# Loads of quads 7 and 8 and half of batch 3's values issued in chunk 1's MLP stage, with an output ring of four

## The chip, the cores and the metric

The kernel runs on one core of one Trainium2 chip. The metric is the device time of one execution in microseconds (us); lower is better. Five engines work side by side and meet through semaphores: PE (TensorE, matmul; its weight loads are a row of their own, PEld), DVE (VectorE), ACT (ScalarE), POOL (GpSimd) and SP (SyncE), which here only issues DMAs. DMAs issued by POOL travel on the queue that the profile calls q0, those of SP on q1; q8 and q14 carry instructions. All use the core's 16 DMA engines.

## The reference

Decayed causal attention for 8 batches x 8 heads, 576 positions, head size 64, followed by an MLP with tanh GELU over all 4608 tokens:

```python
scores = scale * np.matmul(q, k.transpose(0, 1, 3, 2))
cum = np.cumsum(np.log(np.clip(f, 0.0001, 1.0)), axis=-1)
scores = np.where(causal, -1e9, scores + cum[:, :, :, None] - cum[:, :, None, :])
attn = softmax(scores)                 # over the keys
x = matmul(attn, v)  ->  (4608, 512)   # heads side by side
h = x @ w_in                           # 512 x 2048
out = gelu_tanh(h) @ w_out             # 2048 x 512, float32
```

## The kernel before, in words

Attention is done by quads: quad i is four heads of one batch, so batch b is quads 2b and 2b+1, 16 quads in all. The MLP is done by chunks of 512 tokens, nine of them (0 to 8). Chunk c is interleaved with the attention of the two quads that come next: chunk 1 with quads 5 and 6, chunk 2 with quads 7 and 8, and so on.

The order of all work is written by hand. `FRONT` is a string of words for the set-up, chunk 0 and chunk 1; `TABLES[c]` is the like for chunks 2 to 8. `run` and `play` walk over the words, and each word calls one function that emits its instructions, each to the queue of its engine. Every engine works off its own queue in order; a word's place in the string fixes its place in that queue, and semaphores do the rest. The words that matter here:

- `LK.i`, `LQ.i`: load the keys or queries of quad i into `k_c[i % 2]` or `q_c[i % 2]`, turning float32 into bf16, 288 KB written; one DMA, issued by POOL (L190).
- `TK.i`, `TQ.i`: DVE transposes them into `kT`, `qT` (L196). The load of quad i+2 goes into the same buffer as that of quad i, so it waits for the transpose of quad i.
- `LV.b.half`: the values of four heads of batch b, five DMAs on SP (L167), four of 128 KB and one of 64 KB, into half of `v_nat[b % 2]`; packets of 256 bytes. `LX.b.half` is the same issued by POOL. `LV` in a table loads a whole batch (b = c+2), five DMAs of up to 256 KB.
- `@LK.6` and the like, behind a word: it waits for that earlier load to land.
- `S.i.r`: scores of quad i, round r (PE L259, then exp on ACT, L267); `M.i.r`: its causal mask on POOL (L273); `m`: mask by product on DVE (L302); `D.i`: denominators; `V.i.x`: attention times values (L327); `VW.i`, `vw.i`: values weighted, on POOL or DVE (L213).
- `I.c.p` and `P.p`: two of the 16 blocks of the first MLP product of a chunk (PE L372, GELU on ACT L379); `U`, `G`: sums of weights and of GELU outputs on DVE (`w_out` as seven half-size products instead of eight); `F.c.n`, `f.c.n`: the next n of the 112 matmul steps of the second product of chunk c (L508), `O` the rest of the chunk before.

A stage of chunk c from 1 to 5 therefore has an MLP part of some 14 us, in which PE runs 64 long matmuls of 512 columns, and an attention part of some 20 us with short matmuls of many weights: about 700 matmuls and as many weight loads in the stage.

In `FRONT`, chunk 1's MLP stage runs from `I.1.0` to `G.1.1.2`. The words around the change, as they stand before:

```
... LQ.7 VW.4 ... I.1.5 U.1 LV.3.0@LQ.7 m.4.2.2 TK.6 G.0 M.4.0 I.1.2 I.1.3 U.3 ...
... CL.5 m.5.2.2 LQ.8 S.6.0 f.1.10 M.5.1 ... m.6.2.3 LK.7 LK.8 CL.6 LX.3.1@LK.6
```

Stage 2 (`TABLES[2]`) begins with `Y O.512 P.0 P.1 TK.q3 TQ.q3 LK.q5 LQ.q5 TK.q4 TQ.q4 LK.q6 LQ.q6 LV`, where q3 is quad 7, q4 quad 8, q5 quad 9 and q6 quad 10.

Outputs leave through tiles `o_st` of the pool `ostage` (three buffers): DVE adds a PSUM bank and a kept part into `o_st` (L533), SP stores it (L521). The last chunk writes its last corner in pieces (L546, L548). `f_sb` holds the forget gates for the set-up: loaded by SP (L589), clipped on DVE (L605), logarithm on ACT (L606), transposed on PE (L611), and not used after that. `g2` is one of three buffers of sums of GELU outputs (`gsum` in the profile), first written by `G.0` of chunk 1 (L489).

Of the kernel before, what the change touches and what calls it, by code (L numbers as in the profile page):

```python
# [8 lines left out]
FP32 = mybir.dt.float32  # L9
# [7 lines left out]
def kernel(  # L17
# [12 lines left out]
    B, H, S, D = q.shape  # L30
    BH = B * H
# [40 lines left out]

    FRONT = """
        TQ.0 B.2.256 TK.1 SB TR LP.2@LQ.0 B.2.128 CW S.0.0 B.5.384 B.1.256 Z TQ.1 vw.0.0 S.0.2 WI.0 LQ.2 M.0.0 B.3.384 H.1.0.1 LP.3 B.1.256 vw.1.0
        WI.1@LU.4 W H.1.1.1 WI.3 B.2.256 WI.2 H.1.0.0 M.1.0.1 D.0.0 M.1.0.0 H.0.1.1 V.0.0.0 H.0.1.0 B.2.256 M.0.1 H.1.1.0 V.0.1.0 D.1.0 H.0.3.0 B.2.128
        V.1.0.0 LX.1.1 H.0.3.1 V.1.1.0 m.0.3.2 H.1.3.0 m.0.3.4 B.1.256 VW.1.1 H.1.3.1 B.4.128 vw.0.1 D.0.1 M.1.3 S.1.2 M.1.1 LK.2 V.0.1.1 V.0.0.1 WO.0
        J.0.1 D.1.1 J.0.0 WO.1@LV.1.1 V.1.1.1 V.1.0.1 J.0.3 WO.2@WI.1 VW.3 J.1.0 WO.3 LK.3 LQ.3 J.1.1 TQ.2 J.1.3 LQ.4 LX.1.0@WO.2 TK.2 J.0.2 J.1.2 X
        LK.4 F.0.6 TK.3 B.3.256 S.2.0 LK.5 F.0.9 S.2.2 F.0.10 S.2.1 TQ.3 TQ.4 F.0.10 LV.2.0@LK.5 m.2.1 vw.2 TK.4 S.3.0 f.0.1 M.2.2 CL.2 LQ.5 M.2.0 D.2
        f.0.6 S.3.1 m.3.0 F.0.6 V.2.0 S.3.2 TK.5 LK.6 M.3.2 f.0.7 V.2.1 CL.3 S.4.1 m.3.1 LQ.6 F.0.6 TQ.5 H.4.2.1 D.3 H.4.0.1 LQ.7 VW.4 H.4.0.0 V.3.1
        v.3.0 f.0.3 H.4.2.0 CL.4 I.1.0 m.4.1 U.0 LV.2.1@LQ.5 I.1.4 TQ.6 m.4.2.3 I.1.1 I.1.5 U.1 LV.3.0@LQ.7 m.4.2.2 TK.6 G.0 M.4.0 I.1.2 I.1.3 U.3  # L80
        I.1.6 I.1.7 G.1.1.2 U.2 X F.1.16 S.5.0 f.1.26 S.5.1 D.4 M.5.0 f.1.16 S.5.2 V.4.0 m.5.2.3 f.1.10 VW.5 V.4.1 CL.5 m.5.2.2 LQ.8 S.6.0 f.1.10 M.5.1
        D.5 f.1.7 S.6.1 V.5.1 f.1.12 V.5.0 vw.6 S.6.2 m.6.1 M.6.2.2 m.6.0 m.6.2.3 LK.7 LK.8 CL.6 LX.3.1@LK.6
    """

    HOMES = {1: 0, 3: 1}
# [28 lines left out]
    """  # L114

    singles = ctx.enter_context(tc.tile_pool(name="singles", bufs=1))
    ostage_pool = ctx.enter_context(tc.tile_pool(name="ostage", bufs=3))
    snap_pool = ctx.enter_context(tc.tile_pool(name="snap", bufs=4))
    den_pool = ctx.enter_context(tc.tile_pool(name="den", bufs=1))
    rb_pool = ctx.enter_context(tc.tile_pool(name="rb", bufs=2))  # L120
# [4 lines left out]
    def many(n, shape, dtype, name):  # L125
        return [singles.tile(shape, dtype, name=f"{name}{i}") for i in range(n)]
# [11 lines left out]
    vw = many(2, [128, NT + 1, 4, D], BF16, "vw")  # L138
# [4 lines left out]
    g1, g2, g4 = many(3, [128, HF, HC], BF16, "gsum")  # L143
    u1, u2, u4 = many(3, [128, HF, HD], BF16, "usum")
    w_in_sb = singles.tile([128, N_DT, D_FF], BF16, name="w_in_sb")
    w_out_sb = singles.tile([128, N_FT, D_MODEL], BF16, name="w_out_sb")
    f_sb = singles.tile([BH, S], FP32, name="f_sb")
    logfT = singles.tile([128, NT * BH], FP32, name="logfT")
    before = singles.tile([128, (NT - 1) * BH], FP32, name="before")
    wT = singles.tile([128, NQ, NT, 4], FP32, name="wT")  # L150
# [635 lines left out]
```

## Time and profile before

| what | value |
|---|---|
| median of 3 runs | 329.81 us (329.66 to 330.34) |
| the profiled execution, its own time | 329.67 us |
| its span | 328.0 us |
| PE busy | 316.0 us (96%) |
| DVE, ACT, POOL busy | 205.3, 201.7, 110.8 us |
| instruction DMA (q8) | 42 packets, 0.69 MB |
| q0 (POOL's DMAs) | 16.58 MB, 28.3% of 16 engines' span |
| q1 (SP's DMAs) | 16.01 MB, 18.3% |

The span is the time between the first and last instruction that the profile shows; the execution's own time has 1.67 us more around it. Where a row of the profile has "idle before, releaser", the time in brackets is how long that engine had nothing to run, and the name is what ended the wait; "issue" means that nothing in the profile explains it. Queue names ending in q are the engine's sequencer, which issues DMAs and waits. Chunk 1's MLP stage begins at 67.25 us, chunk 2's at 102.01, chunk 3's at 137.11; each is the time of the stage's first matmul of line L372.

### The profile page before, as it was taken

What the parts mean: (1) busy time and instruction counts of PE and PEld (TensorE: products, weight loads), DVE (VectorE), ACT (ScalarE), POOL (GpSimd) and SP (SyncE); (2) the same over time, 40 slices, a digit from 0 to 9 for tenths busy, and PEclk for the clock granted to TensorE, in tenths of its full rate; (3) what the DMA queues carried; (4) which work ended last, traced back from release to release, by engine and by line L of the source; (5) the groups of instructions that cost most, each with busy time, mean ns of one, the idle gap of its engine ahead of it and who ended that gap; (6) DMA issues with size and microseconds to landing.
All of it is one profiled execution on the core that took longest, in us unless ns stands there. A gap on an engine that the chain in (4) does not pass through costs nothing.

```text
span 328.0 us, 11922 instructions
## 1 busy us (share of the span) xinstructions
PE 316.0 (96%) x5395; PEld 206.6 (63%) x5415; DVE 205.3 (63%) x323; ACT 201.7 (61%) x231; POOL 110.8 (34%) x155
## 2 busy tenths in 40 slices
PE   3999999999999999999999999999999999999995
PEld 1358844545776468646774587557754786687684
DVE  4586039894866864674567466636553758785772
ACT  4684677775767576668656774768666841721630
POOL 8986563510414415520644054403440140000000
PEclk9999999999999999999999999999999999999999
DMA  7999999861124990295128711661110102002012
GB/s 125 209 209 218 162 231 201 164 163 35 36 40 95 237 211 27 83 197 110 37 68 179 144 37 36 150 133 36 36 66 0 36 7 96 2 32 98 0 34 96
DMA packets 44322, 33.42 MB, mean 102 GB/s; under 512 B 27488, under 2 KB 37856, under 8 KB 44272
## 3 DMA queue, kind: packets, MB, share of 16 engines
q0 software_dynamic: 8848, 16.58, 28.3%
q1 hardware_dynamic: 35280, 16.01, 18.3%
q8 instruction: 42, 0.69, 0.9%
q14 instruction: 8, 0.07, 0.1%
q10 hardware_dynamic: 144, 0.07, 0.1%
HBM read 36.85 MB, written 9.44 MB: 141 GB/s over the span
## 4 chain that ended last, share of the span: by engine, by line
PE 91%; DMA 3%; POOL 1%; ACT 1%; DVE 1%; issue 1%; DVEq 0%; POOLq 0%; ACTq 0%
PE ps_h L372 29%; PE ps_w L508 29%; PE po L327 9%; PE ps_s L259 8%; PE ps_h L462 4%; PE pso L578 4%; DMA v_nat<-in_v_dram 3%; PE ps_cd L420 2%; PE ps_ab L420 2%; ACT pt L267 1%; PE po_m L313 1%; DMA out_dram<-o_st 1%; POOL v_nat L167 0%; PE ps_o L327 0%; DVE pt L302 0%
## 5 line engine op out<-in xcount | busy, mean ns | idle before, releaser
L267 ACT ACTIVATE pt<-ps_s 128x1024 bf16<-128x1024 f32 (+2 forms) x100 | 93.7, 988 | 39.4 <-PE ps_s L259 34.1
L372 PE MATMUL ps_h<-xT,w_in_sb 128*128 128x512 bf16 x432 | 98.0, 379 | 0.8
L379 ACT ACTIVATE gT<-ps_h 128x1024 bf16<-128x1024 f32 x56 | 57.2, 1021 | 49.1 <-PE ps_h L372 47.6
L273 POOL TENSOR_SCALAR_AFFINE_SELECT pt<-pt 128x512 bf16<-128x512 bf16 (+3 forms) x65 | 38.4, 600 | 133.2 <-ACT pt L267 132.3
L372 PEld LDWEIGHTS <-w_in_sb 128*128 128x128 bf16 x448 | 43.8, 98 | 50.1 <-issue 0.4
L508 PEld LDWEIGHTS <-gT 128*32 128x32 bf16 (+1 forms) x1247 | 51.0, 97 | 6.4 <-issue 1.7
L508 PE MATMUL ps_w<-w_out_sb,gT 128*32 128x256 bf16 (+1 forms) x1050 | 46.9, 273 | 0.0
L508 PEld LDWEIGHTS <-gsum 128*32 128x32 bf16 (+1 forms) x1256 | 38.9, 97 | 1.5 <-issue 0.2
L259 PE MATMUL ps_s<-qT,kT 32*128 32x64 bf16 (+5 forms) x896 | 36.9, 264 | 0.4 <-issue 0.4
L487 DVE TENSOR_TENSOR gsum<-gT 128x1024 bf16<-128x1024 bf16 x16 | 11.0, 689 | 35.2 <-ACT gT L379 35.2
L358 DVE TENSOR_TENSOR xT<-po,rb 128x576 bf16<-128x576 f32 x26 | 19.6, 755 | 20.0 <-PE po L327 19.8
L196 DVE STREAM_TRANSPOSE kT<-k_c 128x576 f32<-128x576 f32 x16 | 19.9, 1246 | 17.6 <-DMA k_c<-in_k_dram 17.6
L508 PE MATMUL ps_w<-usum,gsum 128*32 128x256 bf16 (+1 forms) x832 | 30.6, 273 | 0.0
L213 POOL TENSOR_TENSOR vw<-v_nat,wT 128x1280 bf16<-128x1280 f32 (+1 forms) x13 | 30.3, 2334 | 0.1
L533 DVE TENSOR_TENSOR o_st<-ps_w,snap 128x512 f32<-128x512 f32 x31 | 21.3, 689 | 12.1 <-PE ps_w L508 11.3
L259 PEld LDWEIGHTS <-kT 32*128 32x128 bf16 x896 | 16.9, 93 | 17.6 <-issue 12.8
L327 PE MATMUL po<-pt,vw 128*32 128x64 bf16 (+4 forms) x624 | 22.5, 279 | 0.0
L327 PEld LDWEIGHTS <-vw 128*32 128x32 bf16 x672 | 14.3, 96 | 10.6 <-issue 3.7
L196 DVE STREAM_TRANSPOSE qT<-q_c 128x576 f32<-128x576 f32 x16 | 19.9, 1244 | 1.2 <-PE ps_s L259 0.7
L167 POOL DMA_DIRECT2D v_nat<-in_v_dram x20 | 15.2, 774 | 4.5 <-DMA w_out_sb<-in_moe_w_out_dram 4.5
L508 PE MATMUL ps_w<-usum,gT 128*128 128x256 bf16 (+1 forms) x197 | 16.5, 273 | 0.0
L508 PE MATMUL ps_w<-w_out_sb,gsum 128*32 128x256 bf16 (+1 forms) x400 | 15.4, 273 | 0.0
(100 smaller groups left out, 325.9 us busy)
## 6 DMA issues: line engine op xcount, KB each, us to landing
out_dram<-o_st SPq DMA_DIRECT2D x35, 256.0 KB, 2.3
k_c<-in_k_dram POOLq DMA_DIRECT2D x16, 288.0 KB, 6.5
q_c<-in_q_dram POOLq DMA_DIRECT2D x16, 288.0 KB, 7.6
v_nat<-in_v_dram SPq DMA_DIRECT2D x16, 256.0 KB, 9.0
w_in_sb<-in_moe_w_in_dram POOLq DMA_DIRECT2D x4, 512.0 KB, 9.5
w_out_sb<-in_moe_w_out_dram POOLq DMA_DIRECT2D x4, 512.0 KB, 8.2
v_nat<-in_v_dram SPq DMA_DIRECT2D x16, 128.0 KB, 3.0
v_nat<-in_v_dram POOLq DMA_DIRECT2D x13, 128.0 KB, 7.4
```

The lines of the kernel that those rows point to most:

```text
L167: ins.append(eng.dma_start(out=v_nat[b % 2][:n, t, h0:h0 + nh, :], in_=v[b, h0:h0 + nh, 128 * t:128 * t + n, :].rearrange("h p d -> p h d"),))
L196: nc.vector.transpose(out=dst.rearrange("p s c -> p (s c)").bitcast(FP32) .rearrange("p (t a) -> p a t", a=S // 32), in_=src.rearrange("p ...
L213: eng.tensor_mul(vw[i % 2][:, t0:t1], vb[:, t0:t1, h0:h0 + 4, :], wT[:, i, t0:t1, :].unsqueeze(3).to_broadcast([128, t1 - t0, 4, D]))
L259: nc.tensor.matmul(tiles[h // 2][:, h % 2, c0:c0 + nq], key_columns(i, key, h, c), qq[32 * h:32 * h + 32, q0:q0 + nq, c], start=(c == 0 an ...
L267: nc.scalar.activation(p[:, 2 * g:2 * g + 2, off:off + n], t[:, :, 0:n], AF.Exp, scale=scale)
L273: nc.gpsimd.affine_select(out=x, in_=x, compare_op=ALU.is_ge, fill=0.0, base=0, pattern=pattern, channel_multiplier=-1)
L327: nc.tensor.matmul(po[r0:r0 + w.shape[-1], 448 + q0:448 + q0 + nq], w, p[:, h, col:col + nq], start=(key in (0, "low")), stop=(key in ("lo ...
L358: nc.vector.tensor_mul(xT[:, 2 * u + x, S * b + s0:S * b + s1], po, rbs[i, part])
L372: nc.tensor.matmul(ph[:, j, :], w_in_sb[:, dt, 128 * ft:128 * ft + 128], xT[:, dt, CH * c:CH * (c + 1)], start=(dt == 0), stop=(dt == N_DT ...
L379: nc.scalar.activation(gT[:, 2 * pr:2 * pr + 2, :], ph, AF.Gelu_apprx_tanh)
L508: nc.tensor.matmul(ps[c0:c0 + width, n, cols[0]:cols[1]], x[:, j, 128 * n + c0:128 * n + c0 + width], w[:, j, cols[0]:cols[1]], start=(fir ...
L533: nc.vector.tensor_add(st, ps, kept[name])
```

## The change

Four loads move in `FRONT`, and the buffers change to make room:

- `LK.7`, `LQ.8` and `LK.8` now stand right after `M.4.0`, in chunk 1's MLP stage. Before, `LQ.8` stood in quad 5's attention and the other two at the end of the stage.
- The second half of batch 3's values, five DMAs, was `LX.3.1@LK.6`, the last word of `FRONT`, on POOL. It is now `LV.3.1`, right after `LV.3.0@LQ.7`, on SP, without a gate of its own.
- The ring of output tiles has four buffers instead of three.
- `f_sb` is no longer a tile of its own: it is a view of 64 partitions of `g2` as float32.

PE, DVE and ACT keep the same instructions in the same order. POOL loses five DMA issues and has three others at new places; SP gains five.

```diff
-        v.3.0 f.0.3 H.4.2.0 CL.4 I.1.0 m.4.1 U.0 LV.2.1@LQ.5 I.1.4 TQ.6 m.4.2.3 I.1.1 I.1.5 U.1 LV.3.0@LQ.7 m.4.2.2 TK.6 G.0 M.4.0 I.1.2 I.1.3 U.3
-        I.1.6 I.1.7 G.1.1.2 U.2 X F.1.16 S.5.0 f.1.26 S.5.1 D.4 M.5.0 f.1.16 S.5.2 V.4.0 m.5.2.3 f.1.10 VW.5 V.4.1 CL.5 m.5.2.2 LQ.8 S.6.0 f.1.10 M.5.1
-        D.5 f.1.7 S.6.1 V.5.1 f.1.12 V.5.0 vw.6 S.6.2 m.6.1 M.6.2.2 m.6.0 m.6.2.3 LK.7 LK.8 CL.6 LX.3.1@LK.6
+        LQ.7 VW.4 H.4.0.0 V.3.1 v.3.0 f.0.3 H.4.2.0 CL.4 I.1.0 m.4.1 U.0 LV.2.1@LQ.5 I.1.4 TQ.6 m.4.2.3 I.1.1 I.1.5 U.1 LV.3.0@LQ.7 LV.3.1 m.4.2.2
+        TK.6 G.0 M.4.0 LK.7 LQ.8 LK.8 I.1.2 I.1.3 U.3 I.1.6 I.1.7 G.1.1.2 U.2 X F.1.16 S.5.0 f.1.26 S.5.1 D.4 M.5.0 f.1.16 S.5.2 V.4.0 m.5.2.3
+        f.1.10 VW.5 V.4.1 CL.5 m.5.2.2 S.6.0 f.1.10 M.5.1 D.5 f.1.7 S.6.1 V.5.1 f.1.12 V.5.0 vw.6 S.6.2 m.6.1 M.6.2.2 m.6.0 m.6.2.3 CL.6
...
-    ostage_pool = ctx.enter_context(tc.tile_pool(name="ostage", bufs=3))
+    ostage_pool = ctx.enter_context(tc.tile_pool(name="ostage", bufs=4))
...
-    f_sb = singles.tile([BH, S], FP32, name="f_sb")
+    f_sb = g2.rearrange("p t n -> p (t n)").bitcast(FP32)[0:BH, 0:S]
```

The other lines of `FRONT` are only wrapped anew.

More of the change, by code (lines that the diff above doesn't have):

```diff
@@ L74 @@
         TQ.0 B.2.256 TK.1 SB TR LP.2@LQ.0 B.2.128 CW S.0.0 B.5.384 B.1.256 Z TQ.1 vw.0.0 S.0.2 WI.0 LQ.2 M.0.0 B.3.384 H.1.0.1 LP.3 B.1.256 vw.1.0
-        WI.1@LU.4 W H.1.1.1 WI.3 B.2.256 WI.2 H.1.0.0 M.1.0.1 D.0.0 M.1.0.0 H.0.1.1 V.0.0.0 H.0.1.0 B.2.256 M.0.1 H.1.1.0 V.0.1.0 D.1.0 H.0.3.0 B.2.128
-        V.1.0.0 LX.1.1 H.0.3.1 V.1.1.0 m.0.3.2 H.1.3.0 m.0.3.4 B.1.256 VW.1.1 H.1.3.1 B.4.128 vw.0.1 D.0.1 M.1.3 S.1.2 M.1.1 LK.2 V.0.1.1 V.0.0.1 WO.0
-        J.0.1 D.1.1 J.0.0 WO.1@LV.1.1 V.1.1.1 V.1.0.1 J.0.3 WO.2@WI.1 VW.3 J.1.0 WO.3 LK.3 LQ.3 J.1.1 TQ.2 J.1.3 LQ.4 LX.1.0@WO.2 TK.2 J.0.2 J.1.2 X
@@ L78 @@
-        LK.4 F.0.6 TK.3 B.3.256 S.2.0 LK.5 F.0.9 S.2.2 F.0.10 S.2.1 TQ.3 TQ.4 F.0.10 LV.2.0@LK.5 m.2.1 vw.2 TK.4 S.3.0 f.0.1 M.2.2 CL.2 LQ.5 M.2.0 D.2
-        f.0.6 S.3.1 m.3.0 F.0.6 V.2.0 S.3.2 TK.5 LK.6 M.3.2 f.0.7 V.2.1 CL.3 S.4.1 m.3.1 LQ.6 F.0.6 TQ.5 H.4.2.1 D.3 H.4.0.1 LQ.7 VW.4 H.4.0.0 V.3.1
-        v.3.0 f.0.3 H.4.2.0 CL.4 I.1.0 m.4.1 U.0 LV.2.1@LQ.5 I.1.4 TQ.6 m.4.2.3 I.1.1 I.1.5 U.1 LV.3.0@LQ.7 m.4.2.2 TK.6 G.0 M.4.0 I.1.2 I.1.3 U.3
-        I.1.6 I.1.7 G.1.1.2 U.2 X F.1.16 S.5.0 f.1.26 S.5.1 D.4 M.5.0 f.1.16 S.5.2 V.4.0 m.5.2.3 f.1.10 VW.5 V.4.1 CL.5 m.5.2.2 LQ.8 S.6.0 f.1.10 M.5.1
@@ L82 @@
-        D.5 f.1.7 S.6.1 V.5.1 f.1.12 V.5.0 vw.6 S.6.2 m.6.1 M.6.2.2 m.6.0 m.6.2.3 LK.7 LK.8 CL.6 LX.3.1@LK.6
+        WI.1@LU.4 W H.1.1.1 WI.3 B.2.256 WI.2 H.1.0.0 M.1.0.1 D.0.0 M.1.0.0 H.0.1.1 V.0.0.0 H.0.1.0 B.2.256 M.0.1 H.1.1.0 V.0.1.0 D.1.0 H.0.3.0
+        B.2.128 V.1.0.0 LX.1.1 H.0.3.1 V.1.1.0 m.0.3.2 H.1.3.0 m.0.3.4 B.1.256 VW.1.1 H.1.3.1 B.4.128 vw.0.1 D.0.1 M.1.3 S.1.2 M.1.1 LK.2 V.0.1.1
+        V.0.0.1 WO.0 J.0.1 D.1.1 J.0.0 WO.1@LV.1.1 V.1.1.1 V.1.0.1 J.0.3 WO.2@WI.1 VW.3 J.1.0 WO.3 LK.3 LQ.3 J.1.1 TQ.2 J.1.3 LQ.4 LX.1.0@WO.2 TK.2
@@ new lines @@
+        J.0.2 J.1.2 X LK.4 F.0.6 TK.3 B.3.256 S.2.0 LK.5 F.0.9 S.2.2 F.0.10 S.2.1 TQ.3 TQ.4 F.0.10 LV.2.0@LK.5 m.2.1 vw.2 TK.4 S.3.0 f.0.1 M.2.2
+        CL.2 LQ.5 M.2.0 D.2 f.0.6 S.3.1 m.3.0 F.0.6 V.2.0 S.3.2 TK.5 LK.6 M.3.2 f.0.7 V.2.1 CL.3 S.4.1 m.3.1 LQ.6 F.0.6 TQ.5 H.4.2.1 D.3 H.4.0.1
+        LQ.7 VW.4 H.4.0.0 V.3.1 v.3.0 f.0.3 H.4.2.0 CL.4 I.1.0 m.4.1 U.0 LV.2.1@LQ.5 I.1.4 TQ.6 m.4.2.3 I.1.1 I.1.5 U.1 LV.3.0@LQ.7 LV.3.1 m.4.2.2
+        TK.6 G.0 M.4.0 LK.7 LQ.8 LK.8 I.1.2 I.1.3 U.3 I.1.6 I.1.7 G.1.1.2 U.2 X F.1.16 S.5.0 f.1.26 S.5.1 D.4 M.5.0 f.1.16 S.5.2 V.4.0 m.5.2.3
```

## The prediction

> **What bounds the kernel now.** I read the page's busy shares, then the busy time stage by stage, the chain of waits around the stages that stand out, the DMA view of short windows, and last the timeline of the queues that the change touches. PE is busy for 316.0 of 328.0 us and has 91% of the chain, and the change takes nothing from PE. So the question is where PE stands still. The busy table, cut at the first L372 matmul of chunks 1 to 5 (columns: us, then busy us and count of each engine), tells where:
>
> ```profile
> 67.25:102.01 34.76, 34.48 (x676) 22.20 (x676) 25.72 (x38) 23.99 (x26) 5.32 (x6) 1.00 0.31 75
> 102.01:137.11 35.10, 34.57 (x703) 22.22 (x703) 21.52 (x34) 23.35 (x27) 16.78 (x22) 1.00 0.63 128
> 137.11:171.59 34.48, 34.38 (x703) 22.16 (x703) 21.00 (x32) 23.57 (x27) 12.64 (x16) 1.00 0.48 102
> 171.59:206.06 34.47, 34.37 (x702) 22.13 (x702) 21.06 (x32) 23.58 (x27) 12.63 (x16) 1.00 0.46 102
> ```
>
> Each stretch holds eight L372 groups, two quads of attention and 112 steps of seven products (chunk 1: 107 steps and 5 in the next stage; chunk 2: 100 and 12). Chunks 3 and 4 take 34.48 and 34.47 us, so chunk 2 is 0.62 us too long and chunk 1 0.28 us. The clock is 1.00 in all. The chain has one hole in each of the two, put down to "issue", that is, to no semaphore:
>
> ```profile
> 94.70 0.68 PE po L327 x22
> 95.37 0.17 issue
> 95.54 0.19 PE po L327 x2
> ...
> 120.98 0.13 PE ps_s L259
> 121.11 0.42 issue
> 121.54 0.64 PE ps_s L259 x15
> ```
>
> The reader is to see that PE stops in the middle of a group of equal matmuls, where no operand can be missing. What it may lack is instructions. Queue q8 moves 42 packets of 16 KB on the page, and PE and PEld have 5395 + 5415 rows: 257 rows a packet. Packet by packet in the trace, one goes at 93.12 to 94.08 and one at 119.19 to 120.13; PE resumes at 95.54 and 121.54, 1.46 and 1.41 us after each ends. Both pass through traffic, and chunk 3's counterpart does not. The DMA view of 119.15 to 120.15 (three queues), then of 154 to 156 (one line: q8 alone):
>
> ```profile
> q0 software_dynamic: 77, 0.16, 83.2%
> q1 hardware_dynamic: 112, 0.03, 18.8%
> q8 instruction: 1, 0.02, 5.8%
> ...
> q8 instruction: 1, 0.02, 3.4%
> ```
>
> Counting two rows per weight load, a packet would be asked for about 172 rows into a block of 256. On that count the packets of chunks 3 to 5 start 0.6 to 1.4 us after that point, the one at 93.12 2.1 us and the one at 119.19 2.7 us after it, and PE runs dry about 474 rows into the block. So in chunk 1 a packet was late behind the load of quad 8's queries, and in chunk 2 behind a traffic jam of nearly 19 us.
>
> One rule speaks against this reading. The Trainium skill (Runtime: NRT & Kernel Launch, "Instruction fetch mechanics") says that instructions come in 16 KiB blocks of 256, that PE's store holds 2048 of them, and that crossing a block is mostly hidden. The block size agrees with the trace's 257; a store of 2048 does not agree with a halt some 474 rows into the block. By that rule the holes have another cause; the sum would then be zero (the second rival).
>
> **The change, part by part.** The queues it touches, in the timeline:
>
> ```profile
> 66.18 1.14 POOL L273 TENSOR_SCALAR_AFFINE_SELECT pt<-pt 64x256 bf16<-64x256 bf16 x2
> 86.22 1.47 POOL L273 TENSOR_SCALAR_AFFINE_SELECT pt<-pt 64x256 bf16<-64x256 bf16 x2 [18.90 <-ACT pt L267]
> ...
> 103.19 1.08 POOL L190 DMA_DIRECT2D k_c<-in_k_dram  x2
> 104.26 3.66 POOL L167 DMA_DIRECT2D v_nat<-in_v_dram  x5
> ...
> 68.00 5.77 SPq L167 DMA_DIRECT2D v_nat<-in_v_dram  x10
> ...
> 107.64 1.26 DVE L196 STREAM_TRANSPOSE kT<-k_c 128x576 f32<-128x576 f32 x1 [3.15 <-DMA k_c<-in_k_dram]
> ```
>
> *Three loads into POOL's chunk 1 MLP stage.* Three issues of 0.55 us (L190) are 1.65 us. The first follows the mask that ends at 67.3; the second waits for TQ.6 (DVE, ends 70.5), the third for TK.6 (ends 73.4). Queued behind them is only the mask at 86.22, which waits for ACT: 12 us of cover, cost 0. Without that cover the mask of quad 5 would be late by 0.55 us per load.
>
> *Taken from POOL.* The query load at 90.37 (0.59) goes, and the mask behind it may start 0.6 earlier; ACT and PE do not wait for it: 0. At 103.19 two key loads and five value loads, 1.08 + 3.66 us, go. TK.7 on DVE no longer waits 3.15 us for its keys, so the next pair's loads follow at about 106 instead of 109.19. DVE is not on the chain here: 0.
>
> *Five more issues on SP.* They follow the ten in the trace, with no gate of their own. At 5.77/10 they take 2.9 us, to 76.7; at the pace of chunk 2's value loads under full traffic (11.04 us for five of twice the size, so 1.1 each) all fifteen take 16.6 us, to 84.6. What stands behind them is the first store of chunk 1, at 86.35: cost 0 at both ends.
>
> *The traffic itself, which is the point.* Chunk 1 gets 576 KB of values (1152 to 1728 KB on q1) and three 288 KB loads on q0. By packet time over 16 engines, the ten value loads are 6.0 us, fifteen are 9.0; eight 288 KB equivalents on q0 in chunk 2 are 12.7, so three are 4.8. Together 13.8, and in chunk 3 13.6 us of packets passed in 12.9: traffic runs from 68.2 to about 81.3. The next packet of instructions is asked for at 83.6. Bounds: 80.5 if the queues overlap as in chunk 2 (19.6 us of packets in 17.4), 83.8 if they do not overlap at all (the ten value loads alone took 7.2 us, so 10.8 + 4.8). Even that leaves the packet 0.2 us late, where some 1.9 may be lost. So no new hole in chunk 1, and the old one at 95.37 goes, as nothing is left on q0 then: -0.28 (whole excess) to -0.17 (the hole alone). I take -0.24.
>
> In chunk 2 what is left equals chunk 3's load: four 288 KB loads and 1152 KB of values. SP still starts at 104.98 (the store before it hangs on DVE's add at 103.80, which does not move), and 13.1 us as in chunk 3 is 118.1. The packet is asked for at 116.5, so it is at most 1.6 us late, under the 1.9 or so from which PE halts (by my count of rows; 2.1 gave the hole of 0.17). So -0.62; bounds 0 and -0.62. I take the whole, as chunk 3 carries the same load without a hole.
>
> *Ring of four.* No row of DVE waits for a store except one: the last piece at 323.88, 0.05 us on the chain. -0.05 to 0, taken as 0.
>
> *f_sb in g2.* The same three operations at the start; g2 is first written at 76.81, some 70 us after PE read f_sb: 0. Should the new sharing cost a wait, an already met one on DVE is 21 ns (L533).
>
> What is late next: the three packets after the hole in chunk 2 have 0.2 to 0.5 us to spare, and they gain from an earlier start.
>
> Sum: -0.62 - 0.24 = -0.86. Against the profiled execution, span 328.0 to 327.1 and time 329.67 to 328.81; the median of the runs stands 0.14 higher: 328.95.
>
> **The rivals.** *Half of it.* The traffic of chunk 2 lasts past 118.4, or chunk 1's past 83.6, and a hole of 0.2 to 0.4 is left or made. For it: margins of 0.3 and 2.3 us on an estimate of 13 us. Against it: chunk 3. Time: 329.81 - 0.86 + 0.4 = 329.35, a fall of 0.14%.
>
> *The holes are not from late packets:* PE halts of itself at these places in its program, and nothing moves: 329.8. For it: no row names the cause, and a packet at 126.39 is also 1.5 us late with no traffic beside it. Against it: twice the same 1.4 us between packet and restart. The Trainium skill's rule above would give this time.
>
> *Slower: the jam moves into chunk 1.* The mechanism: under q0's company the value packets keep chunk 2's pace, where 1152 KB took from 104.98 to 121.5. Then 1728 KB take 24.8 us, to 92.8, and three packets of instructions (84.07, 88.10, 93.12) fall into it, each in a phase in which PE runs 256 rows in 3.7 us. At 0.62 each that is 1.86 instead of 0.28; with chunk 2 healed, +1.58 - 0.62 = +0.96: 330.8. It decides from an end of traffic past 88, when at least two holes stand in chunk 1; a first packet as late as at the start of the kernel (4.1 us at 20.61, 2.2 over the limit) would do it alone. For it: five value loads took 16.5 us there. Against it: these had eight loads beside them, not three.
>
> **How the numbers follow.** No change means within 0.2%, 329.15 to 330.47, about what a measurement of this kernel can tell. The forecast has 0.60, with 328.6 (both excesses, the 0.05, and 0.2 of scatter) to 329.15 as its own range; half of it 0.15; nothing 0.07; slower 0.18. So faster 0.60, same 0.22, slower 0.18. For 8 in 10 the range goes from 328.4 (a further 0.2 from the tight packets after the holes) up through the no-change cases to 330.3, leaving out most of the slower rival.
>
> **What would show it, right or wrong.** The stretches of chunks 1 and 2 at about 34.5 each, the "issue" rows of 0.17 and 0.42 gone, q0 and q1 silent from 82 to the first store, no q0 packet between 90 and 95, TK.7 without its 3.15 us. I am wrong if the holes stay with their packets on time, if a hole opens between 84 and 92, or if SP's value issues run into the store at 86.

## The result, and the profile after

| | before | after |
|---|---|---|
| median of 20 runs | 330.40 us (329.66 to 332.13) | 328.26 us (327.57 to 332.39) |
| profiled execution | 329.67 us | 328.08 us |
| its span | 328.0 us | 326.4 us |

The ratio is 0.9935, with a 95% interval of 0.9916 to 0.9954: the change makes the kernel faster, by two and a half times what was forecast. The 20 runs of before, measured beside the change, have a median 0.6 us above that of the three runs that the forecast started from.

The busy table of the kernel after, cut at the first L372 matmul of chunks 1, 2 and 3 (us, then busy us and count of PE, PEld, DVE, ACT, POOL, clock, DMA share, GB/s):

```profile
67.11:101.51 34.40, 34.30 (x675) 22.21 (x676) 25.82 (x38) 23.99 (x26) 6.33 (x8) 1.00 0.52 110
101.51:135.99 34.48, 34.38 (x703) 22.16 (x703) 21.50 (x34) 23.35 (x27) 12.13 (x15) 1.00 0.45 96
135.99:170.45 34.46, 34.35 (x702) 22.12 (x702) 21.00 (x32) 23.57 (x27) 12.65 (x16) 1.00 0.46 102
```

Chunk 1 went from 34.76 to 34.40 us and chunk 2 from 35.10 to 34.48, which is 0.36 and 0.62 us; chunk 3 stayed. Without a hole chunk 1 takes 34.40 us, not the 34.48 of chunk 3. The chain around the two old holes (start, us, what), first near 95 and then near 121 us:

```profile
94.56 0.68 PE po L327 x24
95.24 0.76 PE ps_w L508 x28
...
118.08 2.40 PE ps_w L508 x88
120.48 0.57 PE ps_s L259 x13
```

No "issue" row stands between the pieces any more. The queues that took the loads over, POOL and SP, in the timeline:

```profile
67.13 0.59 POOL L190 DMA_DIRECT2D k_c<-in_k_dram  x1
70.81 0.53 POOL L190 DMA_DIRECT2D q_c<-in_q_dram  x1 [3.08 <-DVE qT L196]
73.67 0.53 POOL L190 DMA_DIRECT2D k_c<-in_k_dram  x1 [2.34 <-DVE kT L196]
86.09 1.47 POOL L273 TENSOR_SCALAR_AFFINE_SELECT pt<-pt 64x256 bf16<-64x256 bf16 x2 [11.89 <-ACT pt L267]
...
67.86 12.20 SPq L167 DMA_DIRECT2D v_nat<-in_v_dram  x15
```

POOL is still idle for 11.89 us behind its loads. SP is through its fifteen issues at 80.1, six microseconds before its next store. Going by the last packets, the moved traffic ends at 82.0 and chunk 2's at 117.7, where the forecast had 81.3 and 118.1.

The two chunks gain 0.36 + 0.62 us, but the two profiled spans differ by 1.6. Matched instruction by instruction, they are 0.13 us apart before chunk 1 and drift 0.11 us more at the end of chunk 6; the rest, 0.35 us, comes after the last store is issued. From there to the end of the span is 3.43 us before and 3.08 us after. SP's own waits in that stretch (engine, line, waited for: us in total, times, longest), before and then after:

```profile
SPq L781 <- DMA out_dram<-o_st: 1.6, 2, 1.5
```

```profile
SPq L781 <- DMA out_dram<-o_st: 1.2, 2, 0.9
```

The trace shows why. The DMAs of SP and ACT take eight semaphores in turn. At the end SP waits for all of them one after another in a fixed order, 0.06 us each when nothing is open. Before, the last two stores had the semaphores first in SP's list, so the checks of all others came after the landing. The change issues five DMAs more there (79 instead of 74), which turns the last two stores to places near the end of that list; the other checks are done while they fly.

### The profile page after: what moved, and what is told of

The parts are those of the page before. It is cut to its first block, busy times and chain, and to the rows that moved or that the text cites. A ratio compares the mean times of both kernels' runs of the same rounds, so it can differ in the third digit from the quotient of the medians.

```text
span 326.4 us, 11918 instructions
## 1 busy us (share of the span) xinstructions
PE 315.5 (97%) x5395; PEld 206.7 (63%) x5415; DVE 205.4 (63%) x323; ACT 201.7 (62%) x231; POOL 107.0 (33%) x150
## 4 chain that ended last, share of the span: by engine, by line
PE 93%; ACT 2%; POOL 2%; issue 1%; DVE 1%; POOLq 0%; DVEq 0%; ACTq 0%
PE ps_w L508 30%; PE ps_h L372 29%; PE po L327 9%; PE ps_s L259 9%; PE ps_h L462 4%; PE pso L578 4%; ACT pt L267 2%; PE ps_cd L420 2%; PE ps_ab L420 2%; PE po_m L313 1%; POOL v_nat L167 1%; PE idle_ps L238 1%; PE ps_o L327 0%; DVE pt L302 0%; PE cum_ps L638 0%
## 5 line engine op out<-in xcount | busy, mean ns | idle before, releaser
L372 PE MATMUL ps_h<-xT,w_in_sb 128*128 128x512 bf16 x432 | 98.1, 379 | 0.8
L372 PEld LDWEIGHTS <-w_in_sb 128*128 128x128 bf16 x448 | 43.8, 98 | 50.1 <-issue 0.4
L508 PEld LDWEIGHTS <-gT 128*32 128x32 bf16 (+1 forms) x1247 | 51.0, 97 | 6.4 <-issue 1.7
L508 PE MATMUL ps_w<-w_out_sb,gT 128*32 128x256 bf16 (+1 forms) x1050 | 46.9, 273 | 0.0
L508 PEld LDWEIGHTS <-gsum 128*32 128x32 bf16 (+1 forms) x1256 | 39.0, 97 | 1.4
L508 PE MATMUL ps_w<-usum,gsum 128*32 128x256 bf16 (+1 forms) x832 | 30.6, 273 | 0.0
L508 PE MATMUL ps_w<-usum,gT 128*128 128x256 bf16 (+1 forms) x197 | 16.4, 273 | 0.0
L578 PE MATMUL pso<-w_out_sb,gT 128*32 128x512 bf16 (+1 forms) x111 | 14.8, 380 | 0.5 <-issue 0.5
L508 PE MATMUL ps_w<-w_out_sb,gsum 128*32 128x256 bf16 (+1 forms) x400 | 15.3, 273 | 0.0
```

What stands on the lines that cost most here:

```text
L372: nc.tensor.matmul(ph[:, j, :], w_in_sb[:, dt, 128 * ft:128 * ft + 128], xT[:, dt, CH * c:CH * (c + 1)], start=(dt == 0), stop=(dt == N_DT ...
L508: nc.tensor.matmul(ps[c0:c0 + width, n, cols[0]:cols[1]], x[:, j, 128 * n + c0:128 * n + c0 + width], w[:, j, cols[0]:cols[1]], start=(fir ...
L578: nc.tensor.matmul(pso[c0:c0 + cols, :], gT[:, ft, 128 * n + c0:128 * n + c0 + cols], w_out_sb[:, ft, :], start=(ft == 0), stop=(ft == N_F ...
```

## The experiments

Two theories were to be told apart at first: PE halts because a packet of its instructions arrives late behind load traffic, or it halts at those places of itself (the second rival of the prediction). Later, two questions of size were added. All ratios are to the kernel before, with 95% intervals.

**The kernel before, again, twice.**

> The kernel before, once more. Theory (late packets of instructions, whose lateness differs from run to run): ratio 1.000 within 0.2%; the holes stand at the same two matmuls near 95 and 121 us, but their lengths differ from 0.17 and 0.42 by more than 0.1 us in at least one. Rival (PE halts there of itself): both holes the same within 0.05 us.

> The kernel before, a third profile. Theory: chunk 2 again 0.5 to 1.0 us too long, chunk 1 anything from 0 to 1.8 us (packet 9 at the limit); last issue to end 3.4 us; ratio 1.000 within 0.2%.

Ratios 1.000 (0.9974 to 1.0026) and 1.0003 (0.9985 to 1.0020). The chain of the first near 95 and 121 us, then that of the second:

```profile
94.59 0.68 PE po L327 x24
95.28 0.76 PE ps_w L508 x28
...
120.64 0.36 issue
```

```profile
95.01 0.68 PE po L327 x22
95.69 0.55 issue
96.23 0.19 PE po L327 x2
...
121.80 0.41 issue
```

The same program has no hole near 95 us in one execution, 0.17 in another and 0.55 in a third. When it is there, the same two matmuls follow it. Chunk 2 of the second was 1.26 us too long, above the 1.0 expected: some 0.6 us at the usual place, and the rest near 126 us, where PE catches up with the next packet of instructions and no "issue" row marks it. In the table, with ring_only and rot_before, which keep the order of these loads, stand all five profiles of it; the unit is us, and chunk 1 is compared with 34.40 and chunk 2 with 34.47. "Too long" is more than the "issue" row alone, as the matmuls around a hole are slower too:

```
             chunk 1  too long   chunk 2  too long   last issue to end
before        34.76     0.36      35.10     0.63         3.43
b_again       34.38     0         35.15     0.68         3.43
b_again2      35.12     0.72      35.73     1.26         3.44
ring_only     34.48     0.08      35.10     0.63         3.43
rot_before    35.41     1.01      35.18     0.71         3.09
mean                    0.43                0.78
after         34.40               34.47                  3.08
loads_only    34.38               34.47                  3.09
rot_after     34.40               34.47                  3.42
a_again       34.40               34.48                  3.11
```

**The order of loads alone, and the buffers alone.**

```diff
 loads_only: the change, but
-bufs=4                       -f_sb = g2.rearrange(...)
+bufs=3                       +f_sb = singles.tile([BH, S], FP32, name="f_sb")
 ring_only: before, with the other two lines instead
```

> The changed order of loads with the old ring of three and f_sb as a tile of its own. Theory: the whole gain, ratio 0.9935 as the change (0.992 to 0.996), no hole in chunks 1 and 2, stages of 34.40 and 34.48 us. Rival (the larger part comes from the ring of four): 0.997 or above.

> The old order of loads with the ring of four and f_sb in g2. Theory: no change, ratio 0.999 to 1.001, both holes there. Rival (ring): 0.997 or below.

0.9963 (0.9946 to 0.9980) and 1.0001 (0.9987 to 1.0015): the ring and f_sb are worth nothing that can be measured, and the moved loads are worth the whole, as a_again (below) confirms with 0.9960 for the full change. The first is above the range I had given it, which was drawn around 0.9935.

**Each half of the move alone.**

```diff
 keys_only:   M.4.0 LK.7 LQ.8 LK.8 I.1.2 ... CL.6 LX.3.1@LK.6
 values_only: LV.3.0@LQ.7 LV.3.1 m.4.2.2 ... LQ.8 S.6.0 ... LK.7 LK.8 CL.6
 q8_only:     M.4.0 LQ.8 I.1.2 ... LK.7 LK.8 CL.6 LX.3.1@LK.6
```

> LK.7, LQ.8 and LK.8 moved as in the change; the half of batch 3's values stays on POOL at the end of FRONT; ring of three, f_sb a tile. Theory: the hole in chunk 1 goes (-0.36 us), chunk 2 has six loads' worth on q0 instead of eight, so its traffic ends at about 119.5 instead of 121.5 and its hole shrinks from 0.6 us to 0 to 0.3 us: ratio 0.996 to 0.998. Rival (the hole is of its place): both stay, ratio 1.000.

> Only the second half of batch 3's values moves, to SP behind LV.3.0; the three loads of keys and queries stay; ring of three. Theory: the hole in chunk 1 stays (LQ.8 is still beside packet 9), chunk 2 loses two loads' worth of q0 traffic, so its hole shrinks from 0.6 us to 0 to 0.3 us: ratio 0.997 to 0.999. Rival (the values are the whole gain): 0.994.

> Only LQ.8 moves, from quad 5's attention into chunk 1's MLP stage. Theory: the hole near 95 us goes and chunk 1 takes 34.40 us, the hole near 121 stays: ratio 0.998 to 0.9995. Rival (the hole is of its place): both holes stay, ratio 1.000.

keys_only 1.0020 (0.9998 to 1.0042), values_only 1.0020 (1.0004 to 1.0036), q8_only 0.9984 (0.9957 to 1.0011). The first hole does as expected: gone without LQ.8 beside it (chunk 1 at 34.40 in keys_only and q8_only), and there with it (36.19 in values_only, whose profiled execution is the slowest of its twelve runs). As b_again also lacks it, the two profiles alone would not show this; in all seven that have LQ.8 moved, chunk 1 takes 34.38 to 34.40. The second does not: I had it shrink with the traffic and both halves gain, but chunk 2 takes 35.49 us in both, 1.0 too long, and neither half is faster. The chain of values_only near 95 and of keys_only near 121:

```profile
95.70 1.31 issue
97.02 0.19 PE po L327 x2
```

```profile
120.87 0.13 PE ps_s L259
121.00 0.71 issue
121.71 0.63 PE ps_s L259 x15
```

In keys_only the last load packet did come earlier, at 121.5 instead of 123.1 us, but the packet of instructions still went only from 119.33 to 120.45, and PE had run dry at 121.00. With the full change the loads end at 117.7 and the packet goes from 116.96 to 118.28, in time. So with less traffic the hole was not shorter in these two profiles, each of which is one draw. I read it so that the loads must be nearly through when the packet is due, and that half a move does not bring them there; no run tests this by itself.

**The same loads, other block boundaries.**

```diff
-B.5.384 B.3.384 B.2.256 (three times) B.3.256
+B.30.64 B.18.64 B.8.64  (three times) B.12.64
```

> The kernel before with its idle matmuls at the start cut into smaller ones: 67 more matmuls and weight loads, 134 rows more of PE ahead of the first scores, so every block boundary falls 134 rows earlier in the work; loads and their order as before. The start may be some us longer. Theory: the holes move with the blocks: none in the scores of S.7.1, where the packet is now asked for in the MLP stage, and the next packet, asked for some 1.9 us sooner than before, inside the traffic, may leave one of up to 0.4 us at about 123.7 us by the old clock; the hole in chunk 1 leaves D.5's matmuls as well. Rival (PE halts at these places of itself): the holes stand at the same two matmuls with the same length.

It was run once, so there is a profile and no ratio. Its chain, over the same stretch:

```profile
120.72 0.56 PE ps_s L259 x15
121.28 0.80 PE po L327 x24
122.08 0.65 PE ps_w L508 x22
122.73 1.61 issue
124.34 1.60 PE ps_w L508 x50
```

The scores of S.7.1 at 120.72 run through, the hole in chunk 1 is gone (34.40 us), and a hole of 1.61 us stands in a group of L508 matmuls where no other profile has one. Its packet went from 121.74 to 122.83 and PE resumed 1.51 us later. The place was forecast to within 1 us, the length was not (0.4 at most). The matmuls at the old places are the same and wait for nothing; only the block boundaries moved. This decides against the rival.

A count over all fourteen profiles says the same. Taking two rows for each weight load, as the prediction did, PE stops after row 2750 near 95 us and after row 3518 near 121 in every profile that has these holes, and after row 3774 in shifted, with 134 rows put in ahead: whole multiples of 256 apart. Nowhere does PE get past one of the rows of this series less than 1.2 us after the end of its packet, and where the packet ended well before, as 2.04 us in b_again near 95, there is no hole.

**A jam made on purpose.**

```diff
 TABLES[3], TABLES[4] of the change:
-... TK.q4 TQ.q4 LK.q6 LQ.q6 LV ... VW.q3 f.18 ...
+... TK.q4 TQ.q4 LV ...             VW.q3 LK.q6 LQ.q6 f.18 ...
```

> The change, with the last two loads of chunks 3 and 4 (LK.q6, LQ.q6) moved out of their MLP stages to stand behind VW.q3 in the attention part. Theory: two loads beside the packet asked for 27.8 us into chunk 3 (26.2 into chunk 4) make it some 2.2 us late, and a hole of 0.1 to 0.6 us opens about 4 us after it in each of the two, with no semaphore to blame: ratio to before 0.995 to 0.997, that is 0.2 to 1.2 us slower than the change. Rival: no hole, 0.9935.

0.9998 (0.9982 to 1.0014), above the range expected: the whole gain is lost again, but not in the way expected. The chain in chunk 4:

```profile
196.17 0.55 POOL k_c L190
196.71 0.53 POOL q_c L190
197.25 1.25 POOL pt L273 x2
198.50 0.04 issue
198.54 0.28 PE po L327 x8
...
202.15 0.43 PE ps_w L508 x13
202.57 0.40 issue
202.97 0.84 PE ps_w L508 x23
```

Here the two loads delay the masks queued behind them on POOL, and PE waits for a mask for 0.28 us; chunk 3 has the same wait of 0.28. That is an ordinary wait, and it muddles the experiment: it makes each of the two chunks 0.5 us longer, and the hole adds about as much once. The 0.40 us further on is the hole that was meant: PE stops after row 7102, of the same series, and resumes 1.44 us after its packet ended at 201.53. In the attention part of chunk 3 the packets ended at least 1.9 us before PE reached their rows, and there is no such hole. So one of the two forecast holes came, where a packet was late, and none where it was not.

**The end of the span, turned on purpose.**

```diff
-"LV": lambda c: load_v(c + 2) if c + 2 < B else None
+rot_before: c == 5: load_v(7, 0, 4) + load_v(7, 4, 4)                 # 10 DMAs, not 5
+rot_after:  c == 5: load_v(7, 0, 4, range(3)) + load_v(7, 4, 4, range(3)) + load_v(7, ts=range(3, NT))   # 8
```

> The kernel before, with batch 7's values (chunk 5) loaded as ten DMAs of half the size instead of five: SP issues five DMAs more in all, as in the change, and nothing else moves. Theory of the end: the DMAs of SP and ACT take eight semaphores in turn, SP's last waits run through them in a fixed order at 0.06 us each, and five more DMAs bring the last store from the first places of that order to the last but one. So the time from the issue of the last store to the end of the span falls from 3.43 to 3.1 us, and the ratio to before is 0.999 (0.9975 to 1.0005, since the holes of chunks 1 and 2 stay). Rival (the shorter end belongs to the ring of four or to chance): 3.4 us stays.

> The change, with batch 7's values loaded as eight DMAs instead of five: three more on SP bring the semaphores' turn back to where it was before (82 DMAs against 74, eight apart). Theory of the end: last issue to end of span 3.43 us again instead of 3.08, stages 1 and 2 at 34.40 and 34.48; 0.35 us slower than the change on the same chip, about 0.1%. Rival: 3.08 stays.

> The change, once more, beside the others. Theory: no hole in chunks 1 and 2, 3.1 us from the last issue to the end; ratio to before 0.994 to 0.997, by how long the holes of before are on this chip: at least 0.98 + 0.35 = 1.3 us, which is 0.996.

SP's waits at the end of rot_before and then rot_after:

```profile
SPq L781 <- DMA out_dram<-o_st: 1.2, 2, 1.0
```

```profile
SPq L781 <- DMA out_dram<-o_st: 1.5, 1, 1.5
```

From the last issue to the end it is 3.09 us in rot_before and 3.42 in rot_after: five DMAs more, issued more than 100 us earlier in another chunk, shorten the end of the kernel before, and three more take that away from the kernel after. In the times it drowns: rot_before 0.9999 (0.9981 to 1.0017), rot_after 0.9963 (0.9950 to 0.9976), a_again 0.9960 (0.9943 to 0.9977), all within expectation but too wide to show 0.1%. The profile of rot_before has 1.01 us too much in chunk 1, so its gain is out of sight there.

## Why the prediction was wrong in size

**Right: where PE stood still and why.** Both holes are packets of instructions that come late behind load traffic. They move with the block boundaries (shifted), and PE resumed 1.2 to 1.5 us after the packet's end in each of them. The rule of the Trainium skill that spoke against it (Runtime: NRT & Kernel Launch, "Instruction fetch mechanics": a store of 2048 instructions for PE, though the same section also speaks of only two lines of 16 KiB) does not describe these traces with its 2048: when a packet starts, at most 286 rows are left before the row at which PE would stop, in any of the fourteen profiles.

**Right: what the moved work costs.** Nothing on POOL, SP or DVE, and the traffic ends where it was put: at 82.0, between the bounds of 80.5 and 83.8. The rival with the jam in chunk 1 needed traffic past 88. Its pace was read wrongly, as the value packets of chunk 2 ended at 123.1 us before the change and not at 121.5; the right pace would have made its jam longer still. The rival of half the gain did not come either.

**Right, but with a margin that was not one: chunk 2's packet "at most 1.6 us late".** The rows pass slowly at the end of the MLP part, so a count that is 20 rows off moves the time at which the packet is asked for by almost 2 us: the row that is 302 before the stop (474 less 172, the prediction's own distance) passes at 114.7 and not at 116.5. What the runs show is that the row is passed 1.6 to 2.6 us after the packet's end in the five profiles with the moved loads, against 1.5 at most where PE halted. The cure holds, with little to spare.

**Wrong: the sum, "-0.62 - 0.24 = -0.86".** Three terms of it.

- Chunk 1's, taken as 0.24 between 0.17 and 0.28, was 0.36 in that same pair of profiles, as chunk 1 without a hole takes 34.40 us and not chunk 3's 34.48.
- Both holes were sized from one execution. Over five profiles chunk 1's is 0 to 1.01 us with a mean of 0.43, chunk 2's 0.63 to 1.26 with a mean of 0.78. The median forecast needed the mean hole, and the range had no room for longer ones on this side: scatter of the holes was counted as 0.2.
- The end of the span had no term. "Five more issues on SP" was costed by its queue alone, and the semaphores that the issues take were not looked at: 0.35 us.

Together 0.43 + 0.78 + 0.35 = 1.56 us, 0.9953 of 329.8. That lies within the intervals of a_again and loads_only and of the result itself, 0.9954 at its edge. The result's 0.9935 is 0.6 us more than this sum. Its runs of before were the longest of all sessions, and longer holes would do it, as in b_again2 (330.97 us with 2.0 us of holes), but those runs were not profiled. Nor does the sum hold the start of the kernel: chunk 1 begins at 67.40 us on average in the five profiles of the old order and at 67.02 in the four of the new, but at 67.70 in jam34, which has the new order there too, so no run shows that the change does this. This remainder stays open.

**Half right: the ring of four at nothing.** ring_only shows no gain. But "-0.05 to 0" was no bound. In shifted, with the ring of three, a store in the last chunk took 3.69 us, and DVE's last piece waited for its buffer; that stretch was 52.68 us long against 51.41 in every other profile, 1.27 more. It happened in one of nine profiles with the ring of three and in none of the five with four.

## What to carry to other kernels

A PE that stops inside a group of equal matmuls with no semaphore to blame may be out of instructions: look for the instruction packet that ended shortly before, and for the loads that were in flight when it was due. Put loads beside long matmuls, where a block of instructions lasts for many microseconds, and have nearly all of the traffic through when the first packet of the dense part is due; half a move brought nothing here. Size such a hole from several profiles, since one execution shows only one draw of it.

## What was not expected of the hardware

The count of DMAs issued by SP and ACT, anywhere in the kernel, changes its last microseconds: with 74 DMAs on SP and ACT the span ends 3.43 to 3.51 us after the last issue (2.98 in shifted, whose last pieces were late and out of step), with 82 it ends 3.42 us after it and with 79 3.08 to 3.12, because the eight semaphores in turn decide which of SP's last checks, 0.06 us each, still follow the last landing.
